# An FFT filter and two MLPs on one core: three weight pairs converted during the filter instead of four, with other load, sign and warm-up places

## The chip, the cores and the metric

The kernel runs on one NeuronCore of a Trainium2 chip. The metric is the device time of one execution in microseconds (us). The kernel before took 1124.01 us in the median of three runs (1123.03 to 1125.35). The execution that the profiler recorded took 1125.17 us; its span, from the first to the last instruction, is 1123.4 us, so 1.77 us lie around the span.

Engines are named as the profile names them: PE is TensorE (PEld its weight loads), DVE is VectorE, ACT is ScalarE, POOL is GpSimd, SP the sync engine, whose queue issues all DMAs here.

## The reference, cut to what matters

```python
x: (2, 3008, 256) float32;  filt_r, filt_i: (1505, 256) float32
w_in: (256, 2048), w_out: (2048, 256), float64, one pair of them for each of two MLPs

X = np.fft.rfft(x, axis=1)
y = np.fft.irfft(X * (filt_r + 1j * filt_i)[None], n=3008, axis=1)     # the filter
t = y.astype(np.float32).reshape(6016, 256)
h = t @ w_in;  t = np.maximum(0.01 * h, h) @ w_out                     # MLP 1
h = t @ w_in2; r = np.maximum(h, 0); t = (r * r) @ w_out2              # MLP 2
```

## The kernel before, in words

**The filter.** 3008 is 47 x 64, so the transform is done as a 47-point and a 64-point one. The 256 channels of two batches make 32 blocks ("units") of 16 channels of one batch. The Python loop at line 686 goes over s = 0 to 35; each s issues one stage of several blocks: `stage_a(s)` (PE, tile pa, 47-point), `stage_b(s-1)` (PE, px, 64-point), `stage_i(s-3)` (PE, zps, inverse 64-point), with `stage_r` (DVE transpose pa to bin), `stage_s` (ACT copies px to xc; DVE multiplies px by the real filter into t1), `stage_2` (POOL multiplies xc by the imaginary filter fi into t2), `stage_y` (t1 + t2 on DVE or POOL, for the 22 blocks in SWAP; the other ten pay a second zps matmul, line 621) and `stage_t` (DVE transpose zps to zin) between them. Channels 0 to 127 are in zin once the first 16 blocks are through, so from s = 19 each step also issues one of 16 `stage_o(0, j)` (PE, pi, four 128-column matmuls, inverse 47-point) and its copy to SBUF (`stage_w`). Two of these go out in each of the last steps (DRAIN). For channels 128 to 255 the 16 `stage_o(1, j)` are issued by `fill()` after the loop; OUT_V names the j that DVE copies, the others are copied by ACT.

**Signs.** Half of the frequencies are read mirrored, so the imaginary filter gets a sign per frequency. `sign_f(q)` does 16 channels in one DVE or POOL multiplication (SGN names the ones for DVE); `sign_k` does one frequency of a range of channels on ACT, 24 of them for a range. SIGN = (q0, q1, first step, how many per step), FI = the ranges (q0, q1, step) in which fi is loaded.

**The MLPs.** Tokens are taken in macros of 1024 (or 960), d_ff in 8 pairs p of 256. One step (macro, pair) does seven products in place of eight (`up`, tiles ph0 to ph3 in PSUM, each one bank and with a single buffer) and four `down` blocks (tiles py). Each float32 operand is split into a high and a low fp32r part, so a product is three matmuls. DVE builds v, u and three h from ph (line 402), ACT applies the activation twice (g and gp), POOL takes the difference (line 391). The first four pairs of macro 0 are done first, then all eight pairs of macro 1, then the rest of macro 0, and so on: pair p = 3 is used by the fourth step, p = 4 to 7 by steps 8 to 11.

**Weights.** They arrive as float64 words, and `narrow_w` (line 194) makes float32 of them on the chip, piece 0 (w_in) and piece 1 (w_out) of a pair apart: `size` (ACT, wm), `upper` (DVE, two instructions), `signed`, `exp`, `low` (DVE), `add` (DVE or POOL), for piece 0 `sums` (four 128 x 128 additions), then `hi` (ACT) and `lo` (DVE or POOL) splits. `load` fetches the raw words of the next pair into the same single buffer, so it comes after `low`.

**The order.** Nothing is reordered at run time: each engine runs its queue in the order of the Python code. `begin(clock, steps, table, start)` gives every step of a table a due tick, start + its number; `tick` (line 289) issues what is due. Clock F ticks four times for each s and once per fill, clock M eight times for each MLP step. Tables: NARROW_F for the pairs converted in the filter (STARTS), NARROW_1 for those in the MLPs (STARTS_1). ON_VECTOR names the steps that go to DVE and not to POOL, by kind (F0 to F3, N1).

**The start.** SP issues the loads in the order of lines 666 to 681 and then of the loop. While the first block is under way, PE runs WARM matmuls on a tile of zeros (line 532).

## Time and profile before

| what | value |
|---|---|
| median of three runs | 1124.01 us |
| profiled execution, its span | 1125.17 us, 1123.4 us |
| PE busy | 1106.2 us (98%) |
| DVE, ACT, POOL busy | 640.2, 659.8, 755.1 us |
| mean granted TensorE clock | 0.995 |
| chain that ended last: PE py, PE ph | 46%, 40% of the span |

The busy shares are means over very different stages. The page's second part cuts the span into 40 slices: PE shows 7 and 8 tenths in the first two slices and 9 (90% or more) in nearly all others; DVE shows 6 to 9 in the first four slices, which are the filter, and 3 to 7 later. The chain that ended last is PE itself from 158.19 us on: every piece of it after that is a ph or a py matmul that begins where the one before it ends. A time in the tables below is in us from the first instruction.

### The profile page before, as it was taken

How to read it: one execution, taken by the hardware profiler on the slowest of the kernel's cores; microseconds unless marked ns; L12 is line 12 of the kernel's file. 1: busy time of each engine (PE TensorE's matmuls, PEld its weight loads, DVE VectorE, ACT ScalarE, POOL GpSimd, SP SyncE). 2: the span in 40 equal slices, each digit the busy share in tenths (PEclk: the TensorE clock that was granted, in tenths of full speed). 3: DMA queues.
4: the chain of work that ended last, by engine and by line, in shares of the span. 5: the costliest groups of instructions: out<-in, count | busy, mean ns of one | idle time of the engine just before them, and what ended most of it. 6: DMA issues, size and time to landing. Idle time of an engine off the chain costs nothing.

```text
span 1123.4 us, 14254 instructions
## 1 busy us (share of the span) xinstructions
PE 1106.2 (98%) x4800; PEld 883.7 (79%) x4800; DVE 640.2 (57%) x873; ACT 659.8 (59%) x1210; POOL 755.1 (67%) x612
## 2 busy tenths in 40 slices
PE   7899999999999999999999999999999999999998
PEld 4466878888888888888888888888888888888887
DVE  6799878866756746746754644434435334334332
ACT  3865566555645645645656766656656556556654
POOL 4685698876866867767768877557547547547544
PEclk8999999999999999999999999999999999999999
DMA  8644622135131221221113220200200200200100
GB/s 232 192 152 131 247 80 76 57 120 162 70 111 38 79 84 38 82 81 38 63 53 115 87 89 1 74 1 1 76 1 1 73 1 1 73 1 1 38 1 35
DMA packets 35240, 80.14 MB, mean 71 GB/s; under 512 B 4544, under 2 KB 14880, under 8 KB 35040
## 3 DMA queue, kind: packets, MB, share of 16 engines
q1 hardware_dynamic: 35168, 79.25, 21.2%
q8 instruction: 37, 0.61, 0.2%
q14 instruction: 35, 0.29, 0.1%
HBM read 51.31 MB, written 27.92 MB: 71 GB/s over the span
## 4 chain that ended last, share of the span: by engine, by line
PE 91%; DVE 3%; POOL 2%; DMA 2%; issue 2%; ACT 1%; SPq 0%; DVEq 0%; POOLq 0%; ACTq 0%
PE py L469 46%; PE ph L368 40%; PE pi L635 2%; DMA xin<-in_x 1%; PE pa L577 1%; PE px L589 1%; PE zps L619 1%; DMA fi<-in_fi 1%; POOL gp L391 0%; DVE zin L628 0%; DVE bin L584 0%; PE zps L621 0%; POOL t L607 0%; DVE t L601 0%; POOL xs L333 0%
## 5 line engine op out<-in xcount | busy, mean ns | idle before, releaser
L391 POOL TENSOR_TENSOR gp<-g,gp 128x512 fp32r<-128x512 f32 (+1 forms) x384 | 506.6, 1324 | 313.1 <-ACT gp L390 98.3
L469 PE MATMUL py<-gp,wao 128*128 128x512 f32 (+1 forms) x1152 | 287.1, 390 | 0.6 <-POOL gp L391 0.6
L469 PE MATMUL py<-gp,wbo 128*128 128x512 f32 (+1 forms) x1152 | 286.6, 391 | 0.0
L469 PEld LDWEIGHTS py<-gp,wao 128*128 128x128 f32 x1152 | 215.9, 187 | 48.6 <-POOL gp L391 1.0
L368 PE MATMUL ph<-xop,wbi 128*128 128x512 f32 (+1 forms) x1008 | 253.9, 390 | 0.0
L368 PE MATMUL ph<-xop,wai 128*128 128x512 f32 (+1 forms) x1008 | 253.8, 391 | 0.0
L469 PEld LDWEIGHTS py<-gp,wbo 128*128 128x128 f32 x1152 | 216.0, 188 | 47.8 <-POOL gp L391 0.3
L368 PEld LDWEIGHTS ph<-xop,wbi 128*128 128x128 f32 x1008 | 189.0, 187 | 41.8
L368 PEld LDWEIGHTS ph<-xop,wai 128*128 128x128 f32 x1008 | 188.9, 188 | 41.6
L402 DVE TENSOR_TENSOR u<-ph,v 128x512 f32<-128x512 f32 (+1 forms) x96 | 65.2, 680 | 176.0 <-PE ph L368 176.0
L381 ACT ACTIVATE g<-h 128x512 f32<-128x512 f32 (+1 forms) x144 | 89.4, 621 | 103.5 <-DVE h L402 102.3
L389 ACT ACTIVATE g<-h 128x512 f32<-128x512 f32 (+1 forms) x144 | 89.2, 619 | 88.2 <-DVE h L398 87.6
L402 DVE TENSOR_TENSOR v<-ph,p 128x512 f32<-128x512 f32 (+1 forms) x96 | 65.0, 678 | 120.7 <-PE ph L368 117.6
L398 DVE CUSTOM_DVE_ANT_0 h<-ph,u 128x512 f32<-128x512 f32 (+1 forms) x96 | 65.2, 680 | 84.0 <-PE ph L368 82.2
L402 DVE TENSOR_TENSOR h<-ph,u 128x512 f32<-128x512 f32 (+1 forms) x96 | 65.1, 679 | 55.0 <-PE ph L368 52.3
L422 ACT ACTIVATE p<-ph 128x512 f32<-128x512 f32 (+1 forms) x96 | 56.2, 586 | 54.8 <-PE ph L368 54.8
L382 ACT ACTIVATE gp<-h 128x512 fp32r<-128x512 f32 (+1 forms) x144 | 87.7, 609 | 0.0
L390 ACT ACTIVATE gp<-h 128x512 fp32r<-128x512 f32 (+1 forms) x144 | 87.7, 609 | 0.0
L387 ACT ACTIVATE r<-ph 128x512 f32<-128x512 f32 (+1 forms) x48 | 28.1, 586 | 68.8 <-PE ph L368 68.7
L381 ACT ACTIVATE g<-ph 128x512 f32<-128x512 f32 (+1 forms) x48 | 28.2, 587 | 59.9 <-PE ph L368 59.9
L344 DVE TENSOR_TENSOR xop<-x,xop 128x512 fp32r<-128x512 f32 (+1 forms) x33 | 49.4, 1497 | 13.4 <-ACT xop L338 7.2
L607 POOL TENSOR_TENSOR t<-xc,fi 128x384 f32<-128x384 f32 x32 | 35.4, 1111 | 24.2 <-ACT xc L597 18.1
(197 smaller groups left out, 1048.2 us busy)
## 6 DMA issues: line engine op xcount, KB each, us to landing
wraw<-in_w SPq DMA_DIRECT2D x32, 512.0 KB
xin<-in_x SPq DMA_DIRECT2D x32, 160.0 KB
xt<-xo SPq DMA_DIRECT2D x26, 188.0 KB
yt<-o SPq DMA_DIRECT2D x16, 256.0 KB
x<-yt SPq DMA_DIRECT2D x4, 1024.0 KB
out<-o SPq DMA_DIRECT2D x16, 256.0 KB
w<-wi SPq DMA_DIRECT2D x8, 448.0 KB
wi<-w SPq DMA_DIRECT2D x8, 448.0 KB
```

What stands on the lines that cost most here:

```text
L344: eng.tensor_tensor(t[:, 1, :n], x_f32[v][name], t[:, 0, :n].bitcast(F32), ALU.subtract)
L368: nc.tensor.matmul(ph[:, :n], w[:, i, k], x[:, j, :n], start=(first and a == 0), stop=(a == 2), skip_group_check=True)
L381: nc.scalar.activation(g[:, :n], h[:, :n], AF.Prelu, alpha=0.01)
L382: nc.scalar.activation(t[:, 0, :n], h[:, :n], AF.Prelu, alpha=0.01)
L389: nc.scalar.activation(g[:, :n], h[:, :n], AF.Square)
L390: nc.scalar.activation(t[:, 0, :n], h[:, :n], AF.Square)
L391: nc.gpsimd.tensor_tensor(t[:, 1, :n], g[:, :n], t[:, 0, :n].bitcast(F32), ALU.subtract)
L398: nc.vector._custom_dve(dve_ops.TENSOR_ADD_SAT, out=t[:, :n], in0=ph[:, :n], in1=s[:, :n], s0=F32_MAX, s1=0.0)
L402: nc.vector.tensor_tensor(t[:, :n], ph[:, :n], s[:, :n], ALU.add)
L422: nc.scalar.activation(p1[:, :n], ph[0][:, :n], AF.Copy)
L469: nc.tensor.matmul(acc[c, t][:, :n], w[:, j, 2 * f + c], g[:, k, :n], start=(p == p0 and f == t and a == 0), stop=(p == p1 - 1 and f != t ...
L607: nc.gpsimd.tensor_tensor(t2, xc, fi_of(units[s][1], units[s][1] + 1), ALU.mult)
```

## The change

The diff does seven things. Names of lines are those of the kernel before unless said otherwise.

1. WARM goes from 12 to 30, and two more matmuls on zeros stand ahead of `stage_a` in s = 1, 2 and 3 (MORE_WARM).
2. The load of piece 1 of pair 0 stands behind the fifth input block instead of ahead of the fourth. The second and third range of fi are loaded one step later each (s = 3 and 8).
3. Signs for q = 4 to 7 (channels 64 to 127) are one DVE multiplication each, at s = 8, 10, 12, 14, and no longer 24 ACT instructions at s = 4 to 9. The other 24, for channels 128 to 255, start at s = 10 instead of 9.
4. Pairs 0, 1 and 2 are converted on clock F, from ticks -10, 64 and 128, each with a table of its own; before, pairs 0 to 3 from -10, 34, 72 and 112 with one table. In the tables for pairs 0 and 1 piece 1 comes later and the steps are further apart.
5. Pair 3 is converted on clock M from tick 0 and pairs 4 to 7 from ticks 28, 40, 52 and 64; before, pairs 4 to 7 from 0, 32, 48 and 64. NARROW_1 itself is the same.
6. In NARROW_1's pairs the four `sums` go to DVE instead of POOL.
7. OUT_V shrinks from nine names to two: seven copies of the fill go from DVE to ACT.

```diff
--- before.py
+++ after.py
@@ -37,31 +37,32 @@
 W_MIN = float(np.uint32(0x38100000).view(np.float32))
 
 
-WARM = 12
+WARM = 30
+MORE_WARM = (0, 2, 2, 2)
 
 
 SWAP = (3, 7, 9, 11, 12, 15, 16, 17, 18, 19, 20, 21, 22, 23, 24, 25, 26, 27, 28, 29, 30, 31)
 SWAP_V = (3, 16, 17, 18, 20, 21, 25, 26, 27, 29, 30)
 
 
-FI = ((2, 4, 2), (4, 8, 2), (8, 16, 7))
-SGN = (1, 2)
-SIGN = ((4, 8, 4, 4), (8, 16, 9, 3))
+FI = ((2, 4, 2), (4, 8, 3), (8, 16, 8))
+SGN = (1, 2, 4, 5, 6, 7)
+SIGN = ((8, 16, 10, 3),)
 
 
 
 H0 = 3
 DRAIN = (2, 2, 2, 2)
 FILLS = 13
-OUT_V = (0, 1, 2, 3, 4, 5, 6, 7, 9)
+OUT_V = (0, 2)
 
 FIN = (0, 0)
 
 
 
 TM = 8
-STARTS = (-10, 34, 72, 112)
-STARTS_1 = (0, 32, 48, 64)
+STARTS = (-10, 64, 128)
+STARTS_1 = (0, 28, 40, 52, 64)
 STARTS_2 = 96
 
 
@@ -69,9 +70,19 @@
 SAVE = dict(b11=2, t2=3, t1=4, b21=5, t3=6, t4=7, b22=8)
 AGAIN = dict(b11=-30, t2=-6, t1=-5, b21=-4, t3=-4, t4=-1, b22=0)
 
-NARROW_F = dict(
-    size0=8, upper0=10, signed0=12, exp0=14, low0=15, add0=18, size1=18, upper1=20, signed1=22, load0=23, sums=23,
...
+NARROW_F = (
+    dict(
+        size0=8, upper0=10, signed0=12, exp0=14, low0=15, add0=18, sums=23, hi_i=30, lo_i=31, size1=34, upper1=41,
...
 NARROW_1 = dict(
     size0=0, upper0=7, signed0=8, exp0=9, low0=11, load0=11, add0=11, size1=12, sums=12, upper1=15, signed1=15, exp1=15,
@@ -96,9 +107,8 @@
 ON_VECTOR = dict(
     F0=(),
     F1=("add0", "lo_o"),
-    F2=("lo_o", "add1"),
-    F3=("add0", "lo_o", "add1"),
-    N1=("add1", "lo_o"),
+    F2=("add0", "lo_o", "add1"),
+    N1=("add1", "lo_o", "sums"),
     N2=(),
     S=("lo_o",),
     M=("lo_b11", "lo_b21", "lo_t2", "lo_t3", "lo_t4"),
@@ -673,19 +683,23 @@
         load_x(2)
         nc.sync.dma_start(ci, c_ci)
         nc.sync.dma_start(cs, c_cs)
-        load_w(0, 0, 1)
         load_x(3)
         load_fr(1)
         load_fi(1, 2)
         load_x(4)
+        load_w(0, 0, 1)
         nc.sync.dma_start(dd, c_dd)
         n = len(units)
         h0 = w0 = 0
         for k, t in enumerate(STARTS):
-            begin("F", narrow_w(0, k, f"F{k}"), NARROW_F, t)
+            begin("F", narrow_w(0, k, f"F{k}"), NARROW_F[k], t)
         for s in range(n + 4):
             if 2 <= s < n - 3:
                 load_x(s + 3)
+            for _ in range(MORE_WARM[s] if s < len(MORE_WARM) else 0):
+                nc.tensor.matmul(
+                    zps[2].rearrange("p c k -> p (c k)")[:, :256], warm[:, :P], warm, start=True, stop=True
+                )
             if s < n:
                 stage_a(s)
             if 1 <= s <= n:
@@ -716,7 +730,7 @@
             for i, (a, b, t) in enumerate(FI):
                 if s == t:
                     load_fi(a, b)
-            if s % 2 == 0 and s // 2 < FI[1][0]:
+            if s % 2 == 0 and s // 2 < SIGN[0][0]:
                 sign_f(s // 2)
             for q0, q1, t, c in SIGN:
                 for k in range(max(0, (s - t) * c), min(NK, (s - t + 1) * c)):
@@ -769,8 +783,8 @@
                 begin("M", {"load": load_part}, {"load": (NP - HALF - 2) * TM}, t)
             else:
                 begin("M", macro_steps(v, "M"), MACRO, t)
-        for p in range(NWA, NP):
-            begin("M", narrow_w(0, p, "N1"), NARROW_1, STARTS_1[p - NWA])
+        for p in range(len(STARTS), NP):
+            begin("M", narrow_w(0, p, "N1"), NARROW_1, STARTS_1[p - len(STARTS)])
         for p in range(NP):
             begin("M", narrow_w(1, p, "N2"), NARROW_2, STARTS_2 + 4 * p * TM)
             begin("M", split_w(1, p, "S", {}), SPLIT_W, ((NM - 1) * NP + p) * TM + LATE[p])
```

The SP queue at the start of the program, before: ci and cs are constants, wraw1 is piece 1 of pair 0, xin the blocks 3 and 4 (two DMAs for a block), fr and fi filter pieces.

```order
L674 DMA ci_114<-in_ci 128x128
L675 DMA cs_115<-in_cs 128x128
L188 DMA wraw1_165<-in_w1 128x1024
L548 DMA xin_167<-in_x 80x512
L548 DMA xin_167<-in_x 14x512
L553 DMA fr_170<-in_fr 128x384
L560 DMA fi0_143<-in_fi 128x384
L548 DMA xin_173<-in_x 80x512
L548 DMA xin_173<-in_x 14x512
L681 DMA dd_117<-in_dd 128x128
```

And now:

```order
L684 DMA ci_114<-in_ci 128x128
L685 DMA cs_115<-in_cs 128x128
L558 DMA xin_183<-in_x 80x512
L558 DMA xin_183<-in_x 14x512
L563 DMA fr_186<-in_fr 128x384
L570 DMA fi0_161<-in_fi 128x384
L558 DMA xin_189<-in_x 80x512
L558 DMA xin_189<-in_x 14x512
L198 DMA wraw1_192<-in_w1 128x1024
L691 DMA dd_117<-in_dd 128x128
```

The weight piece stands six places further back, behind both input blocks.

The DVE queue in an MLP step during which a pair is converted, before (the pair converted from tick 64): u and the first h of the step, then `low` of piece 0 (L228, with wm), then the other two h.

```order
L402 TENSOR_TENSOR u_2202<-ph3_2163,v_2177 128x512 [waits PE_49]
L402 TENSOR_TENSOR h_2204<-ph2_2162,u_2202 128x512 [waits DVE_49]
L228 SCALAR_TENSOR_TENSOR wm_2087<-wraw0_2014,wi32_2180 128x512
L402 TENSOR_TENSOR h_2234<-ph1_2161,u_2202 128x512 [waits PE_49,Activation_49]
L402 TENSOR_TENSOR h_2244<-ph2_2162,v_2177 128x512 [waits DVE_49,PE_49,Activation_49]
L213 TENSOR_SCALAR wm_2219<-wm_2219 128x512 [waits Activation_49]
```

And now, for the pair converted from tick 40. Lines have moved by ten: L412 is u and h, L238 `low`, L251 to L254 the `sums`.

```order
L412 TENSOR_TENSOR u_1893<-ph3_1851,v_1865 128x512 [waits PE_49]
L412 TENSOR_TENSOR h_1895<-ph2_1850,u_1893 128x512 [waits DVE_49]
L238 SCALAR_TENSOR_TENSOR wm_1758<-wraw0_1724,wi32_1871 128x512
L251 TENSOR_TENSOR wi32_1871<-wi32_1871 128x128 [waits Pool_49]
L252 TENSOR_TENSOR wi32_1871<-wi32_1871 128x128 [waits DVE_49]
L253 TENSOR_TENSOR wi32_1871<-wi32_1871 128x128
L254 TENSOR_TENSOR wi32_1871<-wi32_1871 128x128 [waits DVE_49]
L412 TENSOR_TENSOR h_1929<-ph1_1849,u_1893 128x512 [waits PE_49]
L412 TENSOR_TENSOR h_1939<-ph2_1850,v_1865 128x512 [waits PE_49,Activation_49]
```

The four sums stand between `low` and the second h, and the first of them waits for POOL (its `add`, which writes wi32).

The DVE queue at the end of the filter loop, before: zin are the last transposes, t1 the products and additions of the last blocks, wm, wb_, wi32 and wo32 are weight conversion of the fourth pair.

```order
L628 STREAM_TRANSPOSE zin10_679<-zps1_122 128x16x16x2
L614 TENSOR_TENSOR t1_1024<-t1_1024,t2_1039 128x384
L236 TENSOR_TENSOR wi32_1019<-wb__991,wm_983 128x512
L601 TENSOR_TENSOR t1_1048<-px_1033,fr_886 128x384
L213 TENSOR_SCALAR wm_1043<-wm_1043 128x512
L214 TENSOR_SCALAR wb__1064<-wm_1043 128x512
L628 STREAM_TRANSPOSE zin11_120<-zps2_123 128x16x16x2
L217 SCALAR_TENSOR_TENSOR wb__1064<-wraw1_893,wb__1064 128x512
L628 STREAM_TRANSPOSE zin10_679<-zps0_121 128x16x16x2
L222 TENSOR_SCALAR wo32_1088<-wb__1064 128x512
L228 SCALAR_TENSOR_TENSOR wm_1043<-wraw1_893,wo32_1088 128x512
L628 STREAM_TRANSPOSE zin11_120<-zps1_122 128x16x16x2
```

And now, where wm and wb_ belong to the third pair:

```order
L638 STREAM_TRANSPOSE zin10_653<-zps1_122 128x16x16x2
L624 TENSOR_TENSOR t1_986<-t1_986,t2_1000 128x384
L611 TENSOR_TENSOR t1_1006<-px_994,fr_854 128x384
L638 STREAM_TRANSPOSE zin11_120<-zps2_123 128x16x16x2
L638 STREAM_TRANSPOSE zin10_653<-zps0_121 128x16x16x2
L223 TENSOR_SCALAR wm_1035<-wm_1035 128x512
L224 TENSOR_SCALAR wb__1038<-wm_1035 128x512
L638 STREAM_TRANSPOSE zin11_120<-zps1_122 128x16x16x2
L227 SCALAR_TENSOR_TENSOR wb__1038<-wraw0_731,wb__1038 128x512
```

Between the first and the last zin stood six conversion instructions, and now stand two.

## Rows read from the trace of the kernel before

**Rows 1.** The page, chain that ended last, by engine.

```profile
PE 91%; DVE 3%; POOL 2%; DMA 2%; issue 2%; ACT 1%; SPq 0%; DVEq 0%; POOLq 0%; ACTq 0%
```

**Rows 2.** Windows: stretch, length, busy (instructions) per engine, clock, DMA share, GB/s.

```profile
core 0: us, PE busy (x) PEld busy (x) DVE busy (x) ACT busy (x) POOL busy (x), PEclk, DMA share, GB/s
0.00:31.43 31.43, 24.80 (x60) 12.52 (x61) 21.92 (x36) 12.42 (x28) 14.71 (x18) 0.89 0.85 245
31.43:64.81 33.38, 29.90 (x79) 15.22 (x78) 26.52 (x44) 26.75 (x55) 24.87 (x25) 0.95 0.55 167
64.81:106.09 41.28, 40.81 (x184) 26.69 (x182) 39.70 (x65) 21.98 (x45) 28.70 (x28) 1.00 0.43 135
106.09:114.65 8.56, 6.09 (x35) 4.34 (x33) 8.53 (x13) 3.48 (x7) 5.06 (x7) 1.00 0.49 153
114.65:129.02 14.37, 14.37 (x121) 14.37 (x122) 13.23 (x19) 7.61 (x14) 9.61 (x8) 1.00 0.47 150
...
200.00:221.00 21.00, 21.00 (x91) 16.89 (x91) 17.32 (x23) 12.65 (x23) 17.52 (x14) 1.00 0.23 76
```

**Rows 3.** Chain in order of time, filter: start, length, what (PE pieces).

```profile
62.83 0.86 PE pa L577 x2
63.69 0.65 PE px L589 x2
64.33 0.65 PE zps L619 x2
...
70.22 0.93 PE pi L635 x8
```

**Rows 4.** Timeline of PE: start, length, instruction [idle before, what ended it].

```profile
6.48 2.40 PE L577 MATMUL pa<-xin,ra 94*128 94x512 f32 x4 [2.37 <-DMA xin<-in_x]
...
14.52 1.89 PE L577 MATMUL pa<-xin,ra 94*128 94x512 f32 x2 [2.15 <-DMA xin<-in_x]
...
27.12 1.10 PE L577 MATMUL pa<-xin,ra 94*128 94x512 f32 x2
...
45.53 1.62 PE L589 MATMUL px<-bin,cb 128*128 128x384 f32 x2 [2.53 <-DVE bin L584]
...
114.65 14.37 PE L635 MATMUL pi<-dd,zin 128*128 128x128 f32 x120 [1.48 <-DVE zin L628]
```

**Rows 5.** PE windows (busy, clock, DMA share, GB/s) and timeline, the start.

```profile
0.00:12.00 12.00, 8.45 (x22) 0.86 0.76 201
14.80:18.10 3.30, 3.30 (x5) 0.50 0.84 256
...
1.18 2.93 PE L533 MATMUL warm<-warm 128*128 128x256 f32 x12 [1.18 <-DVE warm L528]
```

**Rows 6.** DVE timeline at 41.62; all sign_k instructions (ns min/median/max).

```profile
41.62 0.56 DVE L601 TENSOR_TENSOR t<-px,fr 128x384 f32<-128x384 f32 x1 [2.81 <-ACT xc L597]
...
L573 ACT ACTIVATE fi<-fi,sg x48: 438/528/617, 23.9 to 60.9; 128x64 f32<-128x64 f32 x24, 128x128 f32<-128x128 f32 x24
```

**Rows 7.** DVE timeline at the end of the filter loop.

```profile
108.73 1.21 DVE L614 TENSOR_TENSOR t<-t,t 128x384 f32<-128x384 f32 x1
```

**Rows 8.** Timelines of DVE, POOL and PE in a conversion; PE at 158.19.

```profile
205.09 1.08 DVE L228 SCALAR_TENSOR_TENSOR wm<-wraw,wi 128x512 f32<-128x512 uint32 x1
207.32 0.69 DVE L402 TENSOR_TENSOR h<-ph,u 128x512 f32<-128x512 f32 x1 [1.16 <-PE ph L368]
...
207.80 1.29 POOL L236 TENSOR_TENSOR wi<-wb__1953,wm 128x512 f32<-128x512 f32 x1
209.17 0.53 POOL L241 TENSOR_TENSOR wi<-wi 128x128 f32<-128x128 f32 x1
...
206.36 1.56 PE L368 MATMUL ph<-xop,wai 128*128 128x512 f32 x6
209.16 1.56 PE L368 MATMUL ph<-xop,wbi 128*128 128x512 f32 x6
...
158.19 1.43 PE L469 MATMUL py<-gp,wao 128*128 128x512 f32 x5 [0.56 <-POOL gp L391]
```

More of the change, by code (lines that the diff above doesn't have):

```diff
@@ L70 @@
 AGAIN = dict(b11=-30, t2=-6, t1=-5, b21=-4, t3=-4, t4=-1, b22=0)
-NARROW_F = dict(
-    size0=8, upper0=10, signed0=12, exp0=14, low0=15, add0=18, size1=18, upper1=20, signed1=22, load0=23, sums=23,
-    exp1=26, low1=27, hi_i=30, lo_i=31, add1=32, load1=35, hi_o=38, lo_o=39,
+NARROW_F = (
+    dict(
+        size0=8, upper0=10, signed0=12, exp0=14, low0=15, add0=18, sums=23, hi_i=30, lo_i=31, size1=34, upper1=41,
+        load0=46, signed1=49, exp1=57, low1=65, add1=68, load1=70, hi_o=72, lo_o=74,
+    ),
+    dict(
+        size0=8, upper0=10, signed0=15, exp0=19, low0=23, add0=26, load0=27, sums=28, hi_i=30, size1=30, lo_i=31,
+        upper1=33, signed1=38, exp1=42, low1=46, load1=47, add1=50, hi_o=53, lo_o=55,
+    ),
+    dict(
+        size0=8, upper0=10, signed0=14, size1=14, exp0=16, low0=18, load0=19, add0=20, upper1=22, sums=23, signed1=24,
+        exp1=26, low1=28, add1=29, load1=29, hi_i=30, lo_i=31, hi_o=32, lo_o=34,
+    ),
 )
```

## The prediction

> **What bounds the kernel now.** I read the chain that ended last first, then a table of windows by stage, then TensorE's timeline, then the queues that it waits for. The chain is 91% PE [rows 1]: TensorE sets the end, and the other engines count only where it waits for them. The windows [rows 2] show where that is. From 114.65 us PE is busy all the time (14.37 of 14.37; 21.00 of 21.00 in the MLP stretch), and the change takes no matmul out of the MLPs. So it can gain only in the filter, before 114.65, and can lose anywhere. In the filter PE is busy for 24.80 of 31.43 us, then 29.90 of 33.38, 40.81 of 41.28 and 6.09 of 8.56.
>
> Busy there is not the least time, since a waiting PE also runs slower pieces. A filter step at its densest is pa 0.86, px 0.65 and zps 0.65 [rows 3]: 2.16 us, 2.81 with the second zps matmul, 3.09 with pi (0.93). Against these I set each stage.
>
> The profiled execution took 1125.17 us (span 1123.4 plus 1.77 around it), 1.16 above the median of 1124.01. The sum is made on 1125.17 and the 1.16 is taken off at the end.
>
> **The change part by part.**
>
> *Start, steps 0 to 7.* PE takes block 3 at 14.52 after 2.15 us of waiting for its DMA [rows 4], and block 8 at 31.43, where the second window begins [rows 2]. Up to and with block 3 SP's queue holds 2.41 MB (tile shapes in the order), which is what 201 GB/s move in the first 12.0 us [rows 5]. The 512 KB weight piece leaves this stretch. At 256 GB/s [rows 5] that is 2.0 us, at 201 it is 2.5; I take 2.1, so block 3 starts at 12.4. Steps 3 to 7 need 4 x 2.81 + 2.16 = 13.4 on PE, which would put block 8 at 25.8. But the piece only stands further back: up to block 7 the queue has 5.15 MB instead of 5.66. The same rate from block 3 on gives 14.52 + (5.66 - 2.41)/0.256 = 27.2 before, and the row says 27.12 [rows 4], so the queue sets this stretch; now it gives 12.4 + (5.15 - 1.90)/0.256 = 25.1. One step more is 27.9 for block 8: gain 3.5. Bounds: 2.0 (only block 3's advance) and 5.6 (PE fed all the time).
>
> *Warming.* Twelve matmuls took 2.93 us [rows 5], 0.244 each. Thirty take 7.3 and end at 8.5 at that pace, 2.0 after block 0 starts now (6.48 [rows 4]); at the higher of the two clock levels they would end near 6.5. The stretch 14.8 to 18.1 ran at a granted clock of 0.50 [rows 5], 1.2 GHz, after the wait for block 3, and matmuls in front of it can win that back: half of 3.3 us. A late block 0 has cover, since block 1's products wait for their transposes and block 3 for its DMA. I take 0, between a loss of 2.0 and a gain of 1.6. The six extra ones stand where PE waits for a block or its transpose; without that cover they cost 6 x 0.244 = 1.5. The fi range for channels 64 to 127 now lands behind block 6; its signs begin at s = 8, five steps later, which covers it. The weight piece is used from s = 6.
>
> *Steps 8 to 18.* Eleven steps need 11 x 2.16 + 6 x 0.65 = 27.7; they took 33.38 [rows 2]. The loss of 5.7 is largest where px waits 2.53 us for a DVE transpose [rows 4]: DVE had stood 2.81 us at a product, waiting for ACT's copy xc [rows 6], which is queued behind the signs. Signs take 0.438 to 0.617 us on ACT; those of 64 columns lie at the low end, those of 128 at about 0.53 [rows 6]. The 24 small ones go; at four a step from s = 4, the last eight lie in this stretch: 26.75 - 8 x 0.44 = 23.2 us of ACT work in 27.7, so ACT no longer bounds it. DVE gets four multiplications of about 0.45 and loses conversion steps of F1, which starts 30 ticks later. I leave 1.2 of the 5.7 and take a gain of 4.5. Bounds: 2.0 (the wait at 45.53 shrinks by the eight signs' surplus, and another takes its place) and 5.7.
>
> *Steps 19 to 31.* 13 x 3.09 = 40.2 against 41.28: gain 0.6, between 0 and 1.1.
>
> *Drain.* From 106.09 to 114.65 DVE is busy 8.53 of 8.56 [rows 2] and PE waits for it, at the end 1.48 for zin [rows 4]. PE has there px 0.65, three zps and three pi: 0.65 + 3 x 0.65 + 3 x 0.93 = 5.4. DVE's six conversion instructions between the first and last zin become two. Gain 3.1 (what the chain px, xc, product, addition, zps needs is below what PE needs), between 1.5 and 3.2.
>
> *Fill.* PE is dense; what matters is whether a copy is late. ACT's 14 instructions take 7.61 [rows 2], 0.54 each. Seven more make 11.4 of 14.37; DVE gives up as many, 0.70 each (13.23/19), and gets the third pair's conversion. I take 0; a single late copy costs up to 1.0.
>
> Filter: -(3.5 + 4.5 + 0.6 + 3.1) = -11.7. All at their small ends with the warming at +2.0 it is -3.5, all at the large ones -15.6 and 1.6 more.
>
> *MLPs, sums.* In the row of order quoted, four sums stand between `low` and the h of ph1, and the first waits for POOL's add. Before, such an add ran from 207.80 to 209.09, and h(ph1) ran already at 207.32 [rows 8]. Now DVE, having ended `low`, stands until 209.09, then does four sums. This trace has none on DVE. POOL takes 0.53 [rows 8]; a quarter of the 0.69 of h is 0.17. Bounds 0.15 and 0.53; I take 0.2, since h is the nearest DVE row, and 128 columns are a quarter of its 512. Then h(ph1) runs from 209.9 to 210.6. Behind it stand the other h, and PE's next ph1 product, due 209.86 by the 1.4 us spacing of the ph pieces after 206.36 and 209.16 [rows 8]. PE waits about 0.8, and this comes for pairs 3, 5 and 7, whose conversions start at the same place of a step (ticks 0, 40, 64); with 28 and 52 the sums stand behind v, where nothing is due. Cost 2.4. POOL is relieved of 4 x 0.53 per pair; the one stall of PE on POOL's gp there, 0.56 and its restart at 158.19 [rows 8], goes: -0.7.
>
> *MLPs, closer pairs.* Twelve ticks are 15.75 us a pair, sixteen are 21.0. DVE had 17.32 us in 21.0 [rows 2]; half an MLP step less (five operations of 0.69, halved: 1.7) and sums of 0.9 make 16.5 in 15.75. That is 0.75 over, three times; part of it comes from slack in the buffers, so I take half, 1.2 (0 to 2.3). The raw words are loaded one tick, 1.3 us, before `size` on ACT reads them; 512 KB at 201 GB/s are 2.5 us, and g and gp stand behind `size` on ACT. 0.6 (0 to 2).
>
> MLPs: 2.4 - 0.7 + 1.2 + 0.6 = +3.5, between -1 and +9.
>
> Together -8.2: 1117.0 for the profiled execution, 1115.8 for the median.
>
> **The rivals.**
>
> *A, the sums cost nothing.* POOL, relieved, does the add earlier, and h(ph1) keeps its 1.85 us (from 207.32 to 209.17, when PE's release is still in time). For it: POOL was busy 17.52 of 21.00 [rows 2], so `add` may have stood in a queue. Against it: `low` precedes `add`, and `low` itself ends only at 206.17. MLPs -0.7 to 0, say -0.4: 1125.2 - 12.1 = 1113.1, median 1112.0.
>
> *B, the front stays as it is bounded.* Block 3 is early, but 2.0 is all that comes, and steps 8 to 18 win 2.0, because the larger signs, now from s = 10, still stand ahead of xc. For it: ACT's 26.75 of 33.38 include them; against it: its slack grows. -(2.0 + 2.0 + 0.6 + 3.1) + 3.5 = -4.2: 1121.0, median 1119.8.
>
> *C, slower: DVE becomes the bound in MLP steps 3 to 10.* Each sum costs what it does on POOL: 2.9 of waiting for the add (206.17 to 209.09) and 4 x 0.53 make 5.0 us per pair. DVE then has 17.32 - 1.7 + 5.0 = 20.6 in 15.75: 4.9 late, three times, and 2 for pair 3: 16.6 in place of 3.5 (with the rest of that part in it). -11.7 + 16.6 = +4.9: 1130.1, median 1128.9. It decides as soon as h(ph1) starts more than 1.85 us late in every step. For it: an addition of two operands in SBUF took 1.21 us on DVE for 384 columns [rows 7], while a product with one operand in PSUM took 0.56 [rows 6]; 128 columns at that rate are 0.40. Against it: 0.40 is not 0.53, and DVE has no such wait at pairs 4 and 6.
>
> The Trainium skill, SBUF — State Buffer, section "SBUF: two separate sides", speaks for C: a VectorE instruction with two SBUF inputs and a GpSimd instruction that reads SBUF lock each other out for a whole instruction. The pair of 1.21 and 0.56 agrees with it. By that rule each sum could stand behind one POOL instruction, and C's time would come out; as the sums are short and POOL is relieved of them, I leave it at C's chance.
>
> **How the numbers follow.** Forecast 0.37, A 0.28, B 0.21, C 0.11, something else 0.03. The range leaves out C, and the far end of A: from 1109.0 (A with the drain, middle and start near their large ends) to 1121.5 (B with 1.7 more in the MLPs). A measurement of this kernel can tell 0.2%, 2.25 us, from no change. Slower by more than that is C alone and a little of the rest: 0.11. Within it is B's far end, with MLPs at +6 or more: 0.07. Faster: 0.82.
>
> **What the profile after will show.** Right: block 3's pa near 12.4 and block 8's near 28; no wait of 2.8 us for xc on DVE; the fill's 120 pi starting near 103 instead of 114.65; idle PE of under 1 us at ph1, three times, put down to DVE. Wrong: if the fill starts later than 108, B holds; if PE is dense from 150 to 250, A; if DVE is busy nearly without a gap from 160 to 240 and PE waits for h in every step, C. The thirty warm matmuls still running when block 0 has landed would show the warming as a cost, and a stall of ACT at `size` for raw words the loads as late.

## The result: 1.5% slower

The changed kernel takes 1141.41 us in the median (1138.78 to 1142.07), the kernel before 1124.38 in runs beside it: a ratio of 1.0148, 95% interval 1.0129 to 1.0167. The forecast was 1115.8 (1109.0 to 1121.5). In the profiled executions the span grew from 1123.4 to 1139.8 us, by 16.4.

The chain that ended last is still PE's, with a larger share of DVE (before: [rows 1]):

```profile
PE 86%; DVE 7%; issue 3%; DMA 2%; POOL 1%; ACT 1%; SPq 0%; DVEq 0%; POOLq 0%; ACTq 0%
```

The stages of the changed kernel, cut at the same instructions as [rows 2] (block 8, block 19, the last px, the fill, the first ph), and then the MLPs. Columns: stretch, length, busy time and instructions of PE, PEld, DVE, ACT and POOL, granted clock, DMA share, GB/s.

```profile
0.00:27.94 27.94, 24.55 (x84) 14.61 (x85) 19.40 (x32) 7.41 (x12) 14.03 (x19) 1.00 0.80 230
27.94:56.29 28.35, 28.05 (x80) 14.56 (x78) 25.64 (x42) 21.20 (x42) 18.72 (x18) 1.00 0.66 204
56.29:100.94 44.65, 42.24 (x183) 27.91 (x182) 37.32 (x61) 21.42 (x43) 27.06 (x28) 0.96 0.40 125
100.94:106.34 5.40, 5.40 (x34) 4.36 (x33) 3.86 (x8) 3.39 (x8) 2.74 (x3) 1.00 0.30 107
106.34:121.07 14.73, 14.30 (x121) 14.11 (x120) 13.73 (x17) 8.81 (x20) 10.27 (x10) 1.00 0.44 149
121.07:160.00 38.93, 35.91 (x155) 27.61 (x154) 31.64 (x41) 23.72 (x45) 29.39 (x20) 1.00 0.53 191
160.00:210.00 50.00, 44.48 (x168) 34.05 (x168) 42.05 (x53) 25.98 (x49) 33.24 (x23) 0.90 0.16 53
210.00:260.00 50.00, 44.26 (x175) 34.03 (x174) 40.27 (x55) 24.15 (x44) 27.39 (x19) 0.93 0.16 53
260.00:300.00 40.00, 40.00 (x174) 32.15 (x172) 22.79 (x32) 21.47 (x40) 25.65 (x24) 1.00 0.60 196
```

The fill starts 8.3 us earlier than before (106.34 for 114.65). Then PE, which before waited only 0.56 us in the MLPs, at 158.19 [rows 8], is idle for 3 to 6 us in each of three stretches, and from 260 us on it is dense again. The first ph matmul shows what the filter hands over, in the kernel before and in the changed one:

```profile
128.77 0.94 PE L368 MATMUL ph<-xop,wai 128*128 128x512 f32 x3
```
```profile
121.07 4.05 PE L378 MATMUL ph<-xop,wai 128*128 128x512 f32 x15
```

So the MLPs begin 7.7 us earlier and end 16.4 later: 24.1 us are lost in them, all before 260 us. The longest idle times of PE (start, length, instruction, idle before and what ended it):

```profile
78.48 0.91 PE L599 MATMUL px<-bin,cb 128*128 128x384 f32 x2 [2.11 <-DVE bin L594]
126.32 0.97 PE L378 MATMUL ph<-xop,wai 128*128 128x512 f32 x3 [1.19 <-DVE v L412]
181.60 4.61 PE L479 MATMUL py<-gp,wao 128*128 128x512 f32 x12 [2.06 <-ACT o L505]
203.29 1.65 PE L378 MATMUL ph<-xop,wai 128*128 128x512 f32 x3 [2.61 <-DVE h L412]
231.24 1.65 PE L378 MATMUL ph<-xop,wbi 128*128 128x512 f32 x3 [3.42 <-DVE h L412]
```

And what DVE and POOL did ahead of 203.29:

```profile
196.15 0.68 DVE L412 TENSOR_TENSOR u<-ph,v 128x512 f32<-128x512 f32 x1
196.86 0.69 DVE L412 TENSOR_TENSOR h<-ph,u 128x512 f32<-128x512 f32 x1
197.47 0.68 DVE L238 SCALAR_TENSOR_TENSOR wm<-wraw,wi 128x512 f32<-128x512 uint32 x1
201.49 0.29 DVE L251 TENSOR_TENSOR wi<-wi 128x128 f32<-128x128 f32 x1 [3.34 <-POOL wi L246]
...
202.34 0.29 DVE L254 TENSOR_TENSOR wi<-wi 128x128 f32<-128x128 f32 x1
202.55 0.68 DVE L412 TENSOR_TENSOR h<-ph,u 128x512 f32<-128x512 f32 x1
```
```profile
198.93 1.29 POOL L401 TENSOR_TENSOR gp<-g,gp 128x512 fp32r<-128x512 f32 x1 [2.99 <-DVE wm L238]
200.19 1.27 POOL L246 TENSOR_TENSOR wi<-wb__1839,wm 128x512 f32<-128x512 f32 x1
```

The place is the one that the prediction named. DVE stands 3.34 us at the first sum, since POOL's add is queued behind a difference (gp) for which POOL itself stood idle 2.99 us; then come four sums and only then the h for which PE waits. Over the five pairs that wait is 12.3 us (group of DVE instructions of line 251 up to 262 us: count, busy time, mean ns, idle time before):

```profile
L251 DVE TENSOR_TENSOR wi<-wi 128x128 f32<-128x128 f32 x5 | 3.6, 723 | 12.3 <-POOL wi L246 12.3
```

Ahead of 231.24 it is indirect. A pair's sums began at 220.91, after 1.46 us of waiting, and behind them and the step's first operations stands the pair's second piece: five conversion instructions in a row, 6.1 us, and then the h:

```profile
224.38 1.08 DVE L223 TENSOR_SCALAR wm<-wm 128x512 f32<-128x512 f32 x1
225.49 0.43 DVE L224 TENSOR_SCALAR wb__2112<-wm 128x512 int32<-128x512 int32 x1
225.96 1.69 DVE L227 SCALAR_TENSOR_TENSOR wb__2112<-wraw,wb__2112 128x512 int32<-128x512 int32 x1
227.68 2.18 DVE L232 TENSOR_SCALAR wo<-wb__2112 128x512 int32<-128x512 int32 x1
229.90 0.69 DVE L238 SCALAR_TENSOR_TENSOR wm<-wraw,wo 128x512 f32<-128x512 uint32 x1
230.50 0.68 DVE L412 TENSOR_TENSOR h<-ph,u 128x512 f32<-128x512 f32 x1
```

Ahead of 181.60 ACT stood for raw words that had been asked for one tick before, with its copy of py behind them:

```profile
177.15 0.66 ACT L219 ACTIVATE wm<-wraw 128x512 f32<-128x512 f32 x1
180.40 0.66 ACT L219 ACTIVATE wm<-wraw 128x512 f32<-128x512 f32 x1 [2.60 <-DMA wraw<-in_w]
```

So there were three suspects in the MLPs: the sums, the late raw words and the fifth pair's conversion. After the waits at 181, 203 and 231 the granted clock also fell towards or to its lower level, 1.2 GHz (0.58 from 181.60 to 185.00, 0.50 from 203.29 to 206.00 and from 231.24 to 234.00), a fourth.

### The profile page after: what moved, and what is told of

Same layout as the page of the kernel before. It is cut to its first block, busy times and chain, and to the rows that moved or that the text cites. A ratio compares the mean times of both kernels' runs of the same rounds, so it can differ in the third digit from the quotient of the medians.

```text
span 1139.8 us, 14297 instructions
## 1 busy us (share of the span) xinstructions
PE 1115.5 (98%) x4824; PEld 890.3 (78%) x4824; DVE 654.4 (57%) x890; ACT 652.5 (57%) x1193; POOL 741.2 (65%) x592
## 4 chain that ended last, share of the span: by engine, by line
PE 86%; DVE 7%; issue 3%; DMA 2%; POOL 1%; ACT 1%; SPq 0%; DVEq 0%; POOLq 0%; ACTq 0%
PE py L479 43%; PE ph L378 37%; PE pa L587 1%; PE pi L645 1%; PE px L599 1%; PE zps L629 1%; DVE h L412 1%; DMA fi<-in_fi 1%; POOL wi L246 1%; DMA xop_b<-xop 1%; DVE wm L223 0%; DVE u L412 0%; POOL gp L401 0%; DVE wo L232 0%; DMA wraw<-in_w 0%
## 5 line engine op out<-in xcount | busy, mean ns | idle before, releaser
L378 PE MATMUL ph<-xop,wai 128*128 128x512 f32 (+1 forms) x1008 | 257.5, 393 | 5.7 <-DVE h L412 4.4
L378 PE MATMUL ph<-xop,wbi 128*128 128x512 f32 (+1 forms) x1008 | 256.7, 392 | 5.7 <-DVE h L412 5.7
L412 DVE TENSOR_TENSOR u<-ph,v 128x512 f32<-128x512 f32 (+1 forms) x96 | 65.2, 679 | 171.9 <-PE ph L378 171.8
L412 DVE TENSOR_TENSOR v<-ph,p 128x512 f32<-128x512 f32 (+1 forms) x96 | 64.8, 675 | 118.7 <-PE ph L378 114.7
L412 DVE TENSOR_TENSOR h<-ph,u 128x512 f32<-128x512 f32 (+1 forms) x96 | 65.1, 678 | 48.6 <-PE ph L378 47.0
L354 DVE TENSOR_TENSOR xop<-x,xop 128x512 fp32r<-128x512 f32 (+1 forms) x33 | 49.2, 1492 | 13.5 <-ACT xop L348 8.5
L617 POOL TENSOR_TENSOR t<-xc,fi 128x384 f32<-128x384 f32 x32 | 33.1, 1034 | 28.4 <-ACT xc L607 22.0
```

Of the source, the lines that this page charges most:

```text
L354: eng.tensor_tensor(t[:, 1, :n], x_f32[v][name], t[:, 0, :n].bitcast(F32), ALU.subtract)
L378: nc.tensor.matmul(ph[:, :n], w[:, i, k], x[:, j, :n], start=(first and a == 0), stop=(a == 2), skip_group_check=True)
L412: nc.vector.tensor_tensor(t[:, :n], ph[:, :n], s[:, :n], ALU.add)
L617: nc.gpsimd.tensor_tensor(t2, xc, fi_of(units[s][1], units[s][1] + 1), ALU.mult)
```

## The experiments

Times are medians; ratios are to the kernel before, run beside them, with 95% intervals.

### The sums back on POOL (e1)

```diff
-    N1=("add1", "lo_o", "sums"),
+    N1=("add1", "lo_o"),
```

> The changed kernel with one thing undone: the four sums of a pair converted in the MLPs are on POOL again. Theory 1 (three causes: the sums' wait for POOL's add, raw words that come too late for ACT, two conversions that meet in one step): the stall of PE at ph1 near 203 us (2.61 us and 6.8 us at clock 0.50, together about 6.0) goes, and the small ones near 217 and 245 too; the one near 181 us (behind ACT's copy, about 4.4) and the one near 231 (about 5.9) stay. About 8 us faster than the changed kernel, near 1133. Rival (all of the loss is the sums on DVE): some 20 us faster, near 1121. Second rival (the sums don't matter, POOL becomes late instead): within 2 us of 1141.

1131.28 us (ratio 1.0066, 1.0048 to 1.0083): 10.1 faster than the changed kernel (9.2 by the ratios). The wait at 203 is gone. Of the one at 231, which I had expected to stay, 0.83 us are left: it came from the sums as well. ACT's wait near 181 is still there, and PE waits of 2.03 and 1.22 us at ph, in other steps. The sums are a large part, not the whole.

### Raw words asked for later (e2)

```diff
 NARROW_1 = dict(
-    size0=0, upper0=7, ...
+    size0=4, upper0=7, ...
```

> The changed kernel with size0 at 4 instead of 0 in NARROW_1: ACT asks for the raw words of a pair five ticks (6.5 us) after their load and not one tick after. Theory 1: ACT doesn't stand 2.6 us at its wraw, the py stall near 181 us (2.06 us and 3.4 us at clock 0.50) goes: 4 us faster, near 1137, the stalls at ph1 near 203 and 231 stay. Rival (the sums alone): no difference, 1141.

1139.34 us (1.0135, 1.0115 to 1.0156, which overlaps the interval of the changed kernel: no difference is shown, where 4 us were expected). ACT's wait for the raw words is gone and PE's at py fell to 0.85 us, but the next one at ph, 7 us later, is new:

```profile
180.18 2.36 PE L479 MATMUL py<-gp,wao 128*128 128x512 f32 x9 [0.85 <-DVE o L503]
187.59 0.97 PE L378 MATMUL ph<-xop,wai 128*128 128x512 f32 x3 [1.54 <-DVE h L412]
```

DVE was late there anyway; the wait moved to it.

### The five pairs 16 ticks apart (e3)

```diff
-STARTS_1 = (0, 28, 40, 52, 64)
+STARTS_1 = (0, 16, 32, 48, 64)
```

> The changed kernel with the five pairs of the MLPs begun 16 ticks apart (0, 16, 32, 48, 64). Raw words are then loaded five ticks before use, and no second piece meets a first piece in a step. Theory 1: the stalls near 181 and 231 us go (10 us), those of the sums come once per pair at the same place of a step, each 1 to 6 us: between 1131 and 1141, I take 1136. Rival (the sums alone, with 28 and 52 begun at a harmless place): slower, above 1143, since all five pairs now pay.

1143.08 us (1.0170, 1.0154 to 1.0186): not 5 us faster, which I had expected, but where the rival had it; its interval overlaps that of the changed kernel. Spacing doesn't help while the sums are on DVE; the largest wait of PE is now 3.74 us at 168.62, and each pair after it costs three waits of 0.6 to 1.3 us.

### PE busy in the two longest waits (e4)

```diff
+BUSY = {7: 40, 9: 52}
...
+            for _ in range(BUSY.get(i, 0)):
+                nc.tensor.matmul(acc[0, 0][:, :P], zz, zz, start=False, stop=False, skip_group_check=True)
             product(ph[1], n, w, S2, x["t2"], True)
```

> The changed kernel with 40 and 52 matmuls of 128 columns on zeros, added to an open py accumulation, ahead of ph1 in the two steps in which PE waited 2.61 and 3.42 us for DVE. Nothing comes earlier for it, PE is only busy instead of idle. If the low clock that followed each of these waits (6.8 us at 0.50, worth 3.4 us each) comes from the idle PE, the granted clock stays at 1.00 there and the time falls by about 6.8, to 1134.6. Rival (the low clock has another cause, or idle time alone is the cost): 1141 to 1142, with the low stretches still there.

1140.15 us (1.0144, 1.0126 to 1.0161): no difference. Windows at the two places and 13 us later, first of the changed kernel, then of this one:

```profile
200.00:210.00 10.00, 7.39 (x20) 5.48 (x20) 8.34 (x12) 4.24 (x8) 6.44 (x5) 0.66 0.10 37
229.00:237.00 8.00, 5.76 (x14) 4.57 (x15) 7.73 (x11) 3.19 (x6) 3.22 (x3) 0.57 0.19 66
244.00:252.00 8.00, 7.09 (x31) 5.42 (x30) 7.86 (x11) 4.61 (x8) 5.09 (x4) 1.00 0.01 2
```
```profile
200.00:210.00 10.00, 9.63 (x72) 7.85 (x71) 8.04 (x12) 5.30 (x9) 6.67 (x5) 1.00 0.14 45
229.00:237.00 8.00, 7.31 (x52) 6.03 (x50) 7.93 (x11) 4.29 (x8) 3.97 (x4) 1.00 0.20 68
244.00:252.00 8.00, 7.09 (x24) 5.63 (x25) 7.90 (x10) 4.60 (x8) 5.53 (x4) 0.79 0.00 0
```

The clock stays at 1.00 at both places, as the first theory had it, and the time stays all the same, as the rival had it. DVE is busy 7.7 to 7.9 us of the two windows of 8.0, in both kernels: a faster PE only reaches the next DVE wait sooner (2.63 us at 244.91, and the clock falls there). In these two places the low clock is a consequence of DVE being late, and a slow PE costs nothing while DVE catches up. So the clock was no cause of its own there.

### The add ahead of the sums on DVE too (e8)

```diff
-    N1=("add1", "lo_o", "sums"),
+    N1=("add1", "lo_o", "sums", "add0"),
```

> The changed kernel with the addition ahead of the sums (add of piece 0) on DVE too, so that the sums wait for no other engine. DVE gets 0.68 us more work per pair and loses waits of 1.3 to 3.3 us for POOL. If it is the waiting behind POOL's queue that made the sums cost 10 us, h of ph1 comes about 1.5 to 2.5 us earlier in each of the steps and the time falls to about 1131, as with the sums on POOL. Rival (it is DVE's own work, of which there is now more): 1141 to 1144.

1134.27 us (1.0089, 1.0072 to 1.0106): 7.1 faster than the changed kernel, although DVE does more. The first sum of a pair no longer waits for POOL; the one that stood 3.34 us at 201.49 is now:

```profile
194.64 1.27 DVE L251 TENSOR_TENSOR wi<-wi 128x128 f32<-128x128 f32 x1
```

Most of what the sums cost is the wait behind POOL's queue. About 3 us are left against e1, which has neither the wait nor the sums on DVE, but the two intervals overlap. The run also takes an addition of 1.3 us per pair off POOL, and none parts the two.

### The sums alone, in the kernel before (e6)

The first diff above the other way round, in the kernel before.

> The kernel before with the four sums of its four MLP pairs on DVE, nothing else. If the sums on DVE cost by themselves, each pair loses about 2 us behind POOL's add: near 1132. Rival (they cost only where the pairs lie close together and a fifth is converted): 1124 to 1126.

1133.95 us (1.0089, 1.0074 to 1.0104): 9.7 slower, as expected, for four pairs: 2.4 us each. The first pair shows two waits of PE (1.37 and 0.43 us), each of the other three the same three places; for the third pair:

```profile
215.65 0.96 PE L368 MATMUL ph<-xop,wbi 128*128 128x512 f32 x3 [0.91 <-DVE h L402]
...
224.18 0.96 PE L368 MATMUL ph<-xop,wbi 128*128 128x512 f32 x3 [0.57 <-DVE h L402]
...
227.95 0.97 PE L368 MATMUL ph<-xop,wbi 128*128 128x512 f32 x3 [0.71 <-DVE h L402]
```

The first is the one of the prediction (0.8). The other two come later, where the second piece of the pair, now late, stands ahead of an h.

### Sums on POOL, later size, 16 ticks: the mended kernel (e7)

The edits of e1, e2 and e3 together.

> The changed kernel with the sums on POOL, the pairs of the MLPs 16 ticks apart and size0 at 4: still three pairs converted in the filter and five in the MLPs. If the loss is the sums, the late raw words and the closeness of the pairs, what is left is the 8 us gained by the start of the fill, less about 3.5 in the first two MLP steps, where the extra pair begins: 1120. Rival (a fifth pair is too much for DVE in the MLPs at any spacing): above 1126.

1129.0 us (1.0036, 1.0023 to 1.0049), not 1120. Its fill starts at 104.76, 9.9 us before that of the kernel before, and PE is dense from 182 us on (68.00 of 68.00). All of its loss, 11.3 us from the first ph (119.50, 9.3 early) to the end (2.0 late), lies between 122 and 182. Of PE's waits there 1.4 us fall in the first step (1.19 at 124.73 and 0.24 at 128.28), behind the end of the third filter pair's conversion (DVE's `add` of its piece 1 took 2.62 us at 121.46). The rest lie where the first two pairs of the MLPs meet the splitting of the second macro's operands. The window in the kernel before and in this one, three of the waits, and what DVE did ahead of the first of them, `low` (L238) and two splits of operands (L354):

```profile
160.00:182.00 22.00, 22.00 (x96) 17.71 (x95) 16.26 (x20) 13.93 (x26) 19.54 (x14) 1.00 0.09 32
```
```profile
160.00:182.00 22.00, 15.59 (x58) 11.01 (x57) 19.87 (x23) 12.12 (x22) 20.30 (x16) 0.94 0.21 72
...
163.09 0.96 PE L378 MATMUL ph<-xop,wai 128*128 128x512 f32 x3 [2.26 <-DVE h L412]
...
173.04 0.97 PE L378 MATMUL ph<-xop,wai 128*128 128x512 f32 x3 [1.44 <-DVE h L412]
177.77 0.97 PE L378 MATMUL ph<-xop,wai 128*128 128x512 f32 x3 [1.66 <-DVE h L412]
```
```profile
157.33 1.72 DVE L238 SCALAR_TENSOR_TENSOR wm<-wraw,wi 128x512 f32<-128x512 uint32 x1
158.97 1.79 DVE L354 TENSOR_TENSOR xop<-xs,xop 128x512 fp32r<-128x512 f32 x1
160.68 1.75 DVE L354 TENSOR_TENSOR xop<-x,xop 128x512 fp32r<-128x512 f32 x1
```

DVE is busy 19.87 of 22.00 us (before 16.26, and 17.39 in the stretch 9.3 us later, where the same work stands) and POOL 20.30 (before 19.54 and 17.04): neither has room for a fifth pair in this stretch. With four pairs converted in the filter and the same front, in e9 below, nothing is lost from the first ph to the end (994.65 us against 994.63 before).

### Sums on POOL and later size, starts as in the change (e10)

> The changed kernel with the sums on POOL and size0 at 4, the pairs' starts as in the change. If the late raw words cost ACT 2.2 us and PE with it at 181 us, the time is 3 to 4 us under that of the sums on POOL alone: 1127.5. Rival (DVE is behind there anyway, and the wait only moves): 1130 to 1132.

1131.03 us (1.0057, 1.0039 to 1.0074): nothing won over e1. The raw words were no cause of their own that these runs can tell. From e7 this kernel differs in the starts alone, so the two show what the closer spacing costs once the sums are on POOL: 2.0 us by the medians, with overlapping intervals, and 1.2 from the first ph to the end (12.5 against 11.3). PE's long waits move, from between 187 and 233 us here (2.39, 2.03, 0.84 and 1.22) to between 163 and 178 in e7, and little of them goes.

### The pairs earlier, clear of the second macro (e16)

The mended kernel with

```diff
-STARTS_1 = (0, 16, 32, 48, 64)
+STARTS_1 = (-8, 6, 32, 48, 64)
```

> The changed kernel with sums on POOL, size0 at 4 and the pairs of the MLPs from ticks -8, 6, 32, 48 and 64, so that fewer conversion steps fall into the stretch in which DVE and POOL split the operands of the second macro (150 to 175 us). If it is that meeting that cost 9 us with 0, 16, 32, 48 and 64 (1129.0), some of it goes: 1124 to 1127, I take 1125. Rival (the fifth pair's work on DVE costs the same wherever it is put): 1128 to 1131.

1132.47 us (1.0078, 1.0063 to 1.0094): a miss, above the rival's range too; 3.5 slower than with 0 and 16. PE now waits 2.36 us at 129.79, 2.39 at 145.89 and 3.61 at 173.61, always for h. From the first ph (121.25 in e10, 119.50 in e7, 120.29 in e16) to the end the three spacings with the sums on POOL lose 12.5, 11.3 and 15.9 us; a place without cost was not found, which doesn't show that there is none.

### The front alone (e5), and with a later second piece (e9)

The kernel before with the first three edits of the change (warming, weight piece behind the fifth block, signs and fi). Then the same, with the steps of piece 1 of the first pair put later, so that `size` on ACT comes after its load:

```diff
+PIECE_1 = dict(size1=34, upper1=36, signed1=38, exp1=42, low1=44, add1=48, load1=50, hi_o=56, lo_o=58)
...
-            begin("F", narrow_w(0, k, f"F{k}"), NARROW_F, t)
+            begin("F", narrow_w(0, k, f"F{k}"), NARROW_F | (PIECE_1 if k == 0 else {}), t)
```

> The kernel before with the edits of the start and the signs alone (30 and 6 warming matmuls, the weight piece behind the fifth input block, fi one step later, signs of channels 64 to 127 on DVE); four pairs in the filter, nothing changed in the MLPs. If the start and the signs make most of the filter's gain, the fill begins 5 to 6 us earlier and the MLPs keep it: 1118.5. Rival (the gain of the front is lost behind DVE, which has all of four conversions and four more signs, at the drain): 1122 to 1125.

> The kernel before with the edits of the start and the signs, as in the run of the front alone, but with piece 1 of the first pair converted later (size at 34, upper at 36, and so on, before: 18 and 20), so that DVE doesn't ask for the weight piece that now loads behind the fifth block. Four pairs in the filter, MLPs as before. If the 5.85 us wait at 22.13 us was that weight piece, it goes, and the front's gain stays: block 8 near 28 us, start of the fill 4 to 6 us before 114.65, time 1119 (1117 to 1121). Rival (four conversions leave DVE no room, whatever the start wins is lost by the drain): 1123 to 1126.

e5 took 1131.0 us (1.0057, 1.0042 to 1.0072), e9 1126.62 (1.0020, 1.0011 to 1.0029): both slower, both misses. In e5 PE waits 5.85 us at 22.13 for DVE, which waits for ACT's `size` of the weight piece; e9 mends that, reaches block 8 at 28.57, and loses all of it again to DVE in the next steps:

```profile
42.41 0.88 PE L591 MATMUL px<-bin,cb 128*128 128x384 f32 x2 [2.28 <-DVE bin L586]
...
52.83 0.88 PE L591 MATMUL px<-bin,cb 128*128 128x384 f32 x2 [1.29 <-DVE bin L586]
...
56.61 0.91 PE L591 MATMUL px<-bin,cb 128*128 128x384 f32 x2 [1.39 <-DVE bin L586]
```

### Signs alone (e12), warming alone (e13), start without signs (e14)

e12 has the second edit's fi and the third edit, e13 the first edit, e14 is e9 with signs and fi as before.

> The kernel before with the signs of channels 64 to 127 on DVE, the other signs one step later and fi loaded one step later; nothing else. If ACT's 24 signs were what held up xc in steps 8 to 18, the wait of 2.5 us at 45.5 shrinks and 2 to 4 us are won: 1121. Rival (DVE bounds these steps as soon as ACT doesn't): 1124.

> The kernel before with 30 and six warming matmuls, nothing else. If block 8 waits for its place in the load queue, the warmer clock wins nothing: block 8 stays near 31.4, 1124 (the prediction's 0). Rival (the low clock before 18 us delays the transposes' chain): up to 1.6 faster, 1122.5.

> The kernel before with the start alone: 30 and six warming matmuls, the weight piece behind the fifth input block, piece 1 of the first pair converted later. Four pairs in the filter, signs on ACT and fi as before. If the signs on DVE gave the start's 3 us back (signs alone cost 2.8), the fill begins 2 to 3 us before 114.65: 1122. Rival (DVE has four conversions to do and gives any gain of the start back): 1124 to 1125.

e12: 1127.38 us (1.0025, 1.0016 to 1.0035), a miss: the signs on DVE cost 2.8. e13: 1124.0 (0.9997, 0.9988 to 1.0006), nothing, as forecast; block 8 came at 30.29, 1.1 earlier than I had said, and that was lost again by the first ph (128.84). e14: 1128.32 (1.0038, 1.0026 to 1.0051), a miss again: without the signs the start's gain is lost as well, more of it. With four pairs converted in the filter, steps 8 to 18 take 34.8 us in e12, 38.7 in e14 and 35.0 in e9 (33.4 before, 28.4 in the changed kernel; starts of block 19 less those of block 8).

### The mended kernel with the signs on ACT (e17)

> The mended kernel (three pairs in the filter, sums on POOL, pairs 16 ticks apart) with the signs of channels 64 to 127 and fi as before, on ACT. If the filter's gain in steps 8 to 18 comes from the second pair's later conversion and not from the signs, the time stays at 1129 or falls by up to 2. Rival (the prediction's: ACT's signs hold up xc there): the gain of about 5 us in steps 8 to 18 goes, 1133.

1128.81 us (1.0046, 1.0032 to 1.0059): as the mended kernel. Steps 8 to 18, with ACT 25.93 of 28.34 us busy, still lose next to nothing:

```profile
29.79:58.13 28.34, 27.98 (x79) 14.61 (x78) 23.79 (x40) 25.93 (x56) 19.69 (x19) 1.00 0.61 182
```

They take as long as in the changed kernel (28.35), so the gain there doesn't come from the signs. e14 has the signs on ACT too and takes 38.7; what differs between the two in this stretch is where the conversion steps stand, above all that the second pair starts 30 ticks later.

No version was faster than the kernel before.

## Why the prediction was wrong

Two of its steps failed, both in the MLPs: the sums were priced by the first wait alone, and the fifth pair's conversion stood in the sum at nothing. Term by term, in us, from the stages above:

| term | forecast | measured |
|---|---|---|
| start, to block 8 | -3.5 | 31.43 to 27.94: -3.5 |
| steps 8 to 18 | -4.5 | 33.38 to 28.35: -5.0 |
| steps 19 to 31 | -0.6 | 41.28 to 44.65: +3.4 |
| drain | -3.1 | 8.56 to 5.40: -3.2 |
| fill, to the first ph | 0 | 14.12 to 14.73: +0.6 |
| MLPs | +3.5 | +24.1 |
| sum | -8.2 | +16.4 |

**The start** came out at its number, block 8 at 27.94 for a forecast of 27.9, but not by bytes ahead of the blocks alone. Block 3 starts at 12.56 (forecast 12.4), with the weight piece out of its way. After that PE waits for a block's load only once, 0.33 us at 18.65; the load queue is felt through fi, for which DVE stands 1.71 us at 20.41. Several edits have a part in the 3.5: block 8 comes 1.1 early with the warming alone (e13; the prediction gave it 0, and the 30 matmuls end at 6.55, just ahead of block 0 at 6.59), 1.0 early with the signs and the later fi alone (e12, 30.41), and in e17, which has the new start but not these two, it comes at 29.79, after PE has waited 2.08 us for block 6. How the 3.5 divide is not shown. The 0.5 MB that leave the queue up to block 7 are the second pair's raw words (issued at 29.88 instead of 17.62), since piece 1 itself still stands ahead of block 5.

**Steps 8 to 18** had the right number for a wrong reason, which is luck. The prediction gave the gain to ACT, freed of 24 signs; e17 has them on ACT and the same 28.3 us, e12 has them off ACT, four conversions, and no gain. It is the second pair's conversion that held the steps up: behind the wait for xc in [rows 6] DVE did its first two instructions (0.93 and 1.11 us at 42.09) ahead of the transpose for which PE waited 2.53 us.

**Steps 19 to 31** lost 3.4 where 0.6 was to be won: above all one wait of 2.11 us at 78.48 and a lower clock behind it (0.68 from 78.48 to 82.00). DVE's transpose for it stood behind two instructions of the second pair's second piece (1.33 and 1.10 us at 75.3) and, before these, waits for POOL and ACT. The pair that no longer held up steps 8 to 18 is here now, by these rows (no run moved it away), and the prediction had not looked for it.

**The drain** held with its mechanism: DVE is busy 3.86 of 5.40 us (8.53 of 8.56 before), and PE all of 5.40.

**The sums** failed in size, by a factor of four: 2.4 forecast, 10.1 by e1, 9.7 by e6. The step in words: "this comes for pairs 3, 5 and 7 ... with 28 and 52 the sums stand behind v, where nothing is due". The wait of 0.8 at the first ph was right (0.91 in e6), and a sum was 0.28 to 0.29 us for a forecast of 0.2 (the first of a pair up to 1.37). But DVE works its queue off in order: a wait at the first sum delays everything behind it, the pair's second piece meets an h in the next two steps, and so each pair of e6 pays two or three times. In the changed kernel those that start at 28 and 52 pay too: the wait of 3.42 us at 231.24 follows the sums of the one from 52. The prediction followed the delay to the first h and stopped. POOL's relief (-0.7) came and won nothing: the wait for gp is gone, and near its place PE waits 0.45 us for h, at 152.95.

**The fifth pair** was not priced at all. "Closer pairs" counted busy time over a stretch (16.5 in 15.75 us, 1.2 after halving) and only from pair 5 on. What a whole conversion costs in the first steps, where the second macro's operands are split, was left out; e7, with the other causes mended, still loses 11.3 us in the MLPs, of which some 1.4 are the third filter pair's end. Taken out of the filter, with the other pairs at their new places, it gave 10.7 (the fill starts at 104.76 in e7, at 115.42 in e9, which has the same front and four pairs). Moving the pair is worth nothing even then. The closer spacing itself, the one part that was priced, fits: 1.2 forecast, 1.2 to 2.0 from e10 to e7.

**The raw words** were seen (0.6), had the wait they were said to have (2.60 us on ACT), and cost nothing by themselves that shows: e10 wins nothing without them.

**Rival C** (1128.9, chance 0.11) had the right engine. Its wait of 2.9 us per pair was 2.5 (12.3/5), its price of a sum on DVE (0.53) too high. In the profiled execution its sum was still 11.5 short (1130.1 against 1141.58): 4.0 in the filter, taken over from the forecast, and 7.5 in the MLPs (16.6 against 24.1), since the whole conversion of the fifth pair is in none of the cases.

A and B are out by the prediction's own signs: PE isn't dense from 150 to 250 us, and the fill starts before 108 (106.34; the forecast was near 103).

The common error: DVE was treated as off the path where it was busy for 80% of a stretch. e4 shows the other side of this: with PE made faster in two places nothing is won.

What stays open: whether a fifth pair fits anywhere, as three spacings with the sums on POOL lost 11.3 to 15.9 us; and how the parts add up, since the wider spacing won nothing while the sums were on DVE (e3). The 11.3 belong to the fifth pair, its place and the third filter pair's end together; no run has one of them alone.

## What to carry to other kernels

Work that is moved to an engine which does its queue in order and is some 80% busy should be priced by the whole queue behind it, until it has caught up, and not by the first wait. A wait for another engine's queue was the dearest form of it here: the same four additions, for five pairs, cost 10 us behind a foreign queue and about 3 with their operand made on the same engine. And a gain at the end of one stage is none if it comes from sending work on to the next one, whose busiest engine has no room: here 10.7 us against 11.3.

## What the runs showed of the hardware

In these traces instructions of DVE that only touch SBUF last very differently, and those that read PSUM hardly do. In the changed kernel L412's h from u (one operand in PSUM) has a mean of 686 ns over the 22 up to 262 us, and u, v and h together lie between 0.67 and 0.69 us; one and the same conversion instruction, L232, took 0.43 us at 172.97, where POOL had nothing to do, and 2.18 at 227.68, while POOL was at work:

```profile
172.97 0.43 DVE L232 TENSOR_SCALAR wi<-wb__1684 128x512 int32<-128x512 int32 x1
```
```profile
227.05 2.53 POOL L283 TENSOR_TENSOR wbi<-wi,wbi 128x896 fp32r<-128x896 f32 x1
```

The two POOL and DVE instructions at 227 end within 0.3 us of one another. The Trainium skill, SBUF — State Buffer, section "SBUF: two separate sides", says that an instruction of VectorE, in a mode that uses both ports or with two SBUF inputs against a GpSimd instruction that reads SBUF, and one of GpSimd lock each other out of the ports that they share until the first has ended. These rows agree with it; in which mode L232 runs is not shown, and no run here took one of the two away alone. In any case a conversion has no fixed price on DVE here: L232 took between 0.39 and 2.23 us in the changed kernel, so its row from one place doesn't carry to another.
